# Turning the first four x tiles with plain identity products into fp32 PSUM, in place of transpose-mode instructions

## Chip, cores, metric

One core of a Trainium2 chip (trn2). The metric is the device time of one execution in microseconds (us), median over several executions. "Span" is the time from the first to the last instruction in one profiled execution; it is about 1.7 us shorter than the device time of the same run (163.9 against 165.6 us for the kernel before).

PE is the matmul engine (TensorE), DVE is VectorE, ACT is ScalarE, SP the engine that issues most DMAs (49 of 67 in the trace of the kernel before). PSUM (`ps` in the profiles) is the memory that PE's matmuls write here and that the evictions on DVE and ACT read.

## The reference

The reference mixes two branches of the same x (2048 x 512, bf16) with a gate:

```python
g = sigmoid((x * gate_w).sum(-1, keepdims=True))
a = A_ref(x, A_wqkv, A_wo)        # sliding, dilated attention; starts with x @ wqkv
b = B_ref(x, B_w1, B_b1, B_w2, B_b2)   # layer norm, then an MLP across tokens
return g * a + (1 - g) * b
```

Only `x @ wqkv` matters here. The kernel feeds these matmuls from x with the 512 features on the partitions, in four blocks of 128, that is, from x transposed.

## The kernel before

The kernel is emitted through a small list scheduler: each operation names the resources that it reads and writes ("b5" is PSUM bank 5), and the scheduler fixes an order per engine and the semaphore waits. The x tiles 4 to 15 are transposed by DMA. The first four are too urgent for that (in the trace before, the three DMA transposes land 5.9 to 8.7 us after their issue, the plain loads of x0 to x3 after 2.8 to 4.5): they are loaded plainly, turned on PE, and copied from PSUM to SBUF by DVE (tiles 0 and 2) and ACT (tiles 1 and 3).

```python
def f_warm(e):                      # PE work before any data has arrived
    for n_ in (512,) * 5 + (128,) * 4:
        ins = e.matmul(ps[:, 7, 0:n_], lhsT=C1, rhs=..., start=True, stop=True)

def f_tx(t, k_):                    # two 128x128 blocks of tile t into one bank
    def fn(e):
        for d_ in range(2):
            ins = e.transpose(out=psb(4 + 2 * (t % 2) + k_)[:, d_ * 128:d_ * 128 + 128],
                              in_=X[:, t, (2 * k_ + d_) * 128:(2 * k_ + d_ + 1) * 128], identity=IDENT)
        return ins
    return fn

def xt_ev(t, k_):                   # eviction of that bank to XT, as bf16
    eng = ("dve", "act")[t % 2]
    bk = 4 + 2 * (t % 2) + k_
    src = sub(psb(bk), 0, [(128, 2), (1, 128)])      # psb: the bank seen as bf16
    dst = sub(XT, 2 * k_ * S + t * 128, [(S, 2), (1, 128)])
    ...                             # tensor_copy on DVE, activation Copy on ACT

# ... cut: loads. Order of the DMA queues: x0 wq0 x2 wq2 (SP), x1 wq1 x3 wq3 (ACT), then wk0 wk1 wv x4.. (SP)
pe_tx(0)        # turn tiles 0 and 1: 8 blocks
pe_q0(0, 0)     # query products for their 256 tokens, feature block 0: 4 matmuls of 256 columns
pe_q0(0, 1)
pe_tx(2)        # turn tiles 2 and 3
pe_q0(0, 2)
pe_q0(1, 0); pe_q0(1, 1); pe_q0(1, 2)   # the 256 tokens of tiles 2 and 3
pe_q0(2, 3)     # feature block 3: 4 matmuls of 512 columns
# ... cut: key and value projections (512 columns each), attention, MLP, output
```

Of the kernel before, what the change touches and what calls it, by code (L numbers as in the profile page):

```python
# [280 lines left out]
class _Mem:  # L281
# [17 lines left out]
    def view(self, name, dtype, dims, extra=0, p0=0, np_=128):  # L299
        base = self.arena[:].bitcast(dtype)  # L300
        pst = base.ap[0][0]
        esz = mybir.dt.size(dtype)
        o = self.off[name]
        assert o % esz == 0
        return bass.AP(base.tensor, p0 * pst + o // esz + extra, [[pst, np_]] + [list(d) for d in dims])


def bass_gated_mix__sliding_local_dilated__mixer_token_mlp__prompt_kernel(nc, A_x, A_wqkv, A_wo, B_x, B_w1, B_b1, B_w2, B_b2, gate_w, out, dbg=None):
    with contextlib.ExitStack() as es:
# [37 lines left out]
        ps = es.enter_context(nc.psum_tensor("ps", [128, 8, 512], FP32))  # L347
# [11 lines left out]
        X = view("X", BF16, [(D, NST), (1, D)])  # L359
# [40 lines left out]
        IDENT = view("IDENT", BF16, [(1, 128)])  # L400
# [38 lines left out]
        def psb(bank):  # L439
            return ps[:, bank, :].bitcast(BF16)  # L440

        def sub(ap_, offs, dims):
            return bass.AP(ap_.tensor, ap_.offset + offs, [list(ap_.ap[0])] + [list(d) for d in dims])

        def psub(ap_, p0, np_, offs, dims):
            pst = ap_.ap[0][0]
            return bass.AP(ap_.tensor, ap_.offset + p0 * pst + offs, [[pst, np_]] + [list(d) for d in dims])
# [4 lines left out]
        def act(o_, i_, f_, **kw):  # L452
            return lambda e: e.activation(out=o_, in_=i_, func=f_, **kw)  # L453
# [109 lines left out]
        def f_tx(t, k_):  # L563
            def fn(e):
                ins = None
                for d_ in range(2):
                    ins = e.transpose(out=psb(4 + 2 * (t % 2) + k_)[:, d_ * 128:d_ * 128 + 128],  # L567
                                      in_=X[:, t, (2 * k_ + d_) * 128:(2 * k_ + d_ + 1) * 128], identity=IDENT)
                return ins
            return fn  # L570

# [2 lines left out]
        def xt_ev(t, k_):  # L574
            eng = ("dve", "act")[t % 2]
            bk = 4 + 2 * (t % 2) + k_
            src = sub(psb(bk), 0, [(128, 2), (1, 128)])
            dst = sub(XT, 2 * k_ * S + t * 128, [(S, 2), (1, 128)])
            extl[eng] = A(eng, (lambda e: e.tensor_copy(out=dst, in_=src)) if eng == "dve" else act(dst, src, AF.Copy),  # L579
                          0.27 if eng == "dve" else 0.35, reads=["b%d" % bk], writes=["xt0_%d_%d" % (t, k_)], name="ext%d_%d" % (t, k_), prio=-30)  # L580
# [12 lines left out]
        def pe_tx(t):  # L593
            for k_ in range(2):
                for t_ in (t, t + 1):
                    PE(f_tx(t_, k_), 0.2, ["x%d" % t_, "ident"], ["b%d" % (4 + 2 * (t_ % 2) + k_)], "tx%d_%d" % (t_, k_))
                    xt_ev(t_, k_)
# [133 lines left out]
        for h in range(2):  # L731
# [55 lines left out]
            for c in range(4):  # L787
                src = psub(ATT[h], 32 * c, 32, 0, [(0, 4), (1, NW * UT_)])
# [230 lines left out]
```

## Time and profile before

| | before |
|---|---|
| device time, 3 runs | 165.26 us (165.26 to 165.47) |
| span of the profiled run | 163.9 us |
| PE busy | 97% of the span |
| turning of the four tiles and first query products | 3.7 to 9.5 us |

From the page of the kernel before: the busy times (engine, us, share of the span, number of instructions), then the chain of work that ended last, by engine.

```profile
PE 159.3 (97%) x793; PEld 77.5 (47%) x808; DVE 150.7 (92%) x126; ACT 70.2 (43%) x100; POOL 12.0 (7%) x36
...
PE 95%; DMA 2%; ACT 1%; issue 1%; DVE 0%
```

PE is busy nearly throughout, and 95% of the chain is PE: what holds PE up lengthens the kernel. From the costliest groups of the same page (line, engine, operation, destination and source, count; then busy us and mean ns of one; then idle time before them and what ended it):

```profile
L579 DVE COPY arena<-ps 128x256 bf16<-128x256 bf16 x4 | 1.1, 291 | 4.4 <-PE ps L567 4.2
...
L588 PE MATMUL ps<-arena 128*128 128x256 bf16 (+1 forms) x27 | 4.4, 313 | 0.2
```

The evictions on DVE are bf16 to bf16, 291 ns each. The 27 query matmuls (24 of 256 columns, and three of the four of 512, one of which the trace lacks) average 313 ns, partly because some of them ran at a slow clock, as the next view shows. It is the timeline of the kernel before from 3.2 to 7.2 us, merged by line: start, length, engine, line, operation, count, and in brackets the idle time before it and what ended it. A group that runs on past 7.2 us is counted only up to there. PEld is the load of the stationary operand that goes ahead of a matmul (for the first query matmul at 4.86, ahead of 4.89 us).

```profile
3.74 1.01 PE L567 MATMUL ps<-arena 128*128 128x128 bf16 x8 [0.17 <-DMA arena<-in_A_x_dram]
4.15 0.72 DVE L579 COPY arena<-ps 128x256 bf16<-128x256 bf16 x2 [2.46 <-PE ps L567]
4.36 0.81 ACT L453 ACTIVATE arena<-ps 128x256 bf16<-128x256 bf16 x2 [0.37 <-PE ps L567]
4.86 1.37 PEld L588 LDWEIGHTS ps<-arena 128*128 128x128 bf16 x8 [0.38 <-DVE arena L579]
4.89 1.61 PE L588 MATMUL ps<-arena 128*128 128x256 bf16 x8
...
6.33 0.61 PE L567 MATMUL ps<-arena 128*128 128x128 bf16 x8
6.65 0.51 DVE L579 COPY arena<-ps 128x256 bf16<-128x256 bf16 x2 [1.78 <-PE ps L567]
...
6.76 0.66 ACT L453 ACTIVATE arena<-ps 128x256 bf16<-128x256 bf16 x2 [1.58 <-PE ps L567]
6.78 0.60 PE L588 MATMUL ps<-arena 128*128 128x256 bf16 x4
```

Read it as a staircase: eight transposes, evictions on DVE and ACT, eight query matmuls, eight transposes, evictions, more query matmuls. Single instructions of the same trace add three things. Transposes start 107 ns apart in the first group and 56 ns apart in the second. Query matmuls of 256 columns start 213 ns apart until about 6.1 us and 109 ns apart afterwards. "The clock doubles" is a name for this change below: it is read from the distances between starts, because the granted clock that the profile lists is 1.00 over these same first 10 us. And x0 landed at 3.60 us, x3 at 6.22, wq2 (the third block of the query weights) at 6.65.

### The profile page before, as it was taken

Reading aid. Unit: us, or ns where it says so; the run is one execution under the profiler, and the core shown is the slowest. Engines: PE = TensorE matmul, PEld = TensorE weight load, DVE = VectorE, ACT = ScalarE, POOL = GpSimd, SP = SyncE. Lnnn points to the kernel's source line nnn. Section 1 sums busy time; section 2 is a strip of 40 time slices with the busy share of each in tenths; the row PEclk is TensorE's granted clock in tenths of the full one; section 3 lists DMA queues with packets and bytes.
Section 4 is the critical chain, followed back from the end, with each engine's and each line's share of the span. In section 5 each row is a group of like instructions: output and inputs, shape, how many; then the busy total and the mean of one; then the engine's idle time right before and its main releaser. Section 6 shows DMA issues by size and latency. Waiting matters only on the chain.

```text
span 163.9 us, 1989 instructions
## 1 busy us (share of the span) xinstructions
PE 159.3 (97%) x793; PEld 77.5 (47%) x808; DVE 150.7 (92%) x126; ACT 70.2 (43%) x100; POOL 12.0 (7%) x36
## 2 busy tenths in 40 slices
PE   7999999999999999999999999999999999999993
PEld 3755555555544444444444344444444444444641
DVE  0589989999999999999999999999999999999971
ACT  3357677766672379753111258111121111111164
POOL 3000021020000000004000000002200222000000
DMA  4999969909499094999998974990998799991014
GB/s 153 288 233 253 254 128 291 199 11 188 91 304 308 1 247 120 256 290 290 298 263 233 270 203 142 298 232 10 283 254 192 185 204 201 211 222 38 32 58 135
DMA packets 44684, 32.24 MB, mean 197 GB/s; under 512 B 7940, under 2 KB 42244, under 8 KB 44676
## 3 DMA queue, kind: packets, MB, share of 16 engines
q1 hardware_dynamic: 41444, 22.06, 51.9%
q0 software_dynamic: 2512, 9.44, 27.2%
q10 hardware_dynamic: 720, 0.62, 1.1%
q8 instruction: 6, 0.10, 0.2%
q14 instruction: 2, 0.02, 0.0%
HBM read 18.88 MB, written 2.10 MB: 128 GB/s over the span
## 4 chain that ended last, share of the span: by engine, by line
PE 95%; DMA 2%; ACT 1%; issue 1%; DVE 0%
PE ps L858 29%; PE ps L885 29%; PE ps L649 23%; PE ps L894 8%; PE ps L588 3%; DMA arena<-in_A_x_dram 2%; PE ps L722 1%; ACT arena L453 1%; PE ps L567 1%; PE ps L717 1%; DVE arena L579 0%; PE ps L604 0%
## 5 line engine op out<-in xcount | busy, mean ns | idle before, releaser
L450 DVE TENSOR_TENSOR arena<-arena 128x4096 bf16<-128x4096 bf16 (+8 forms) x79 | 132.0, 1718 | 1.9 <-ACT arena L453 0.6
L885 PE MATMUL ps<-arena 128*128 128x512 bf16 (+2 forms) x234 | 50.0, 366 | 0.2
L858 PE MATMUL ps<-arena 128*128 128x512 bf16 x218 | 48.5, 379 | 0.3
L453 ACT ACTIVATE arena<-ps,arena 128x512 bf16<-128x512 f32 (+1 forms) x30 | 21.8, 731 | 60.7 <-PE ps L894 37.7
L453 ACT ACTIVATE arena<-ps 128x512 bf16<-128x512 f32 (+3 forms) x53 | 32.9, 629 | 18.3 <-PE ps L649 10.9
L649 PE MATMUL ps<-arena 128*128 128x512 bf16 x173 | 38.0, 379 | 0.2
L885 PEld LDWEIGHTS ps<-arena 128*128 128x128 bf16 x238 | 22.8, 98 | 25.9
L858 PEld LDWEIGHTS ps<-arena 128*128 128x128 bf16 x224 | 21.7, 98 | 26.8 <-issue 0.8
L649 PEld LDWEIGHTS ps<-arena 128*128 128x128 bf16 x176 | 19.9, 113 | 18.0
L894 PE MATMUL ps<-arena 128*128 128x512 bf16 (+2 forms) x67 | 15.6, 366 | 0.1
L453 ACT ACTIVATE arena<-arena 128x16 f32<-128x16 f32 (+5 forms) x10 | 6.7, 678 | 9.7 <-DVE arena L450 9.7
L692 DVE BATCH_NORM_STATS2 arena<-arena 128x6 f32<-128x512 bf16 x16 | 9.9, 679 | 0.5 <-DMA arena<-in_A_x_dram 0.5
L954 ACT ACT_TABLE_LOAD x7 | 9.0, 1283 | 2.8 <-issue 2.7
L894 PEld LDWEIGHTS ps<-arena 128*128 128x128 bf16 x68 | 6.5, 98 | 7.3
L790 POOL DMA_DIRECT2D arena<-arena x8 | 4.3, 556 | 75.2 <-DVE arena L450 75.2
L706 DVE TENSOR_SCALAR arena<-arena 128x512 bf16<-128x512 bf16 x16 | 5.3, 406 | 0.0
L579 DVE COPY arena<-ps 128x256 bf16<-128x256 bf16 x4 | 1.1, 291 | 4.4 <-PE ps L567 4.2
L827 POOL DMA_DIRECT2D arena<-arena x3 | 3.6, 1209 | 17.7 <-DVE arena L450 17.7
L747 POOL DMA_DIRECT2D arena<-arena x2 | 2.5, 1268 | 31.5 <-DVE arena L692 21.5
L588 PE MATMUL ps<-arena 128*128 128x256 bf16 (+1 forms) x27 | 4.4, 313 | 0.2
L588 PEld LDWEIGHTS ps<-arena 128*128 128x128 bf16 x28 | 3.1, 119 | 1.1 <-DVE arena L579 0.4
L551 PE MATMUL ps<-const-bfloat16-1.0 128*128 128x512 bf16 (+1 forms) x9 | 2.7, 483 | 0.8 <-PEq L1004 0.8
(30 smaller groups left out, 14.4 us busy)
## 6 DMA issues: line engine op xcount, KB each, us to landing
arena<-in_B_w_dram SPq DMA_DIRECT2D x7, 1024.0 KB, 6.5
arena<-in_B_w_dram SPq DMA_DIRECT2D x8, 896.0 KB, 9.9
arena<-arena POOLq DMA_DIRECT2D x5, 1024.0 KB, 10.0
arena<-arena POOLq DMA_DIRECT2D x8, 512.0 KB, 11.7
out_dram<-arena SPq DMA_DIRECT2D x15, 128.0 KB, 2.3
arena<-in_A_x_dram SPq DMA_DIRECT2D x3, 512.0 KB, 4.7
arena<-in_A_wqkv_dram SPq DMA_DIRECT2D x2, 256.0 KB, 4.3
arena<-in_A_wqkv_dram SPq DMA_DIRECT2D x1, 512.0 KB, 6.5
```

Source lines behind the costliest of these rows:

```text
L450: return lambda e: e.tensor_tensor(out=o_, in0=a_, in1=b_, op=op_)
L453: return lambda e: e.activation(out=o_, in_=i_, func=f_, **kw)
L588: ins = e.matmul(ps[:, dl, c0:c1], lhsT=sub(WQKV, dt * 3 * D + dl, [(4, 128)]), rhs=XT[:, dt, c0:c1], start=(dt == 0 and hb == 0), stop=(d ...
L649: ins = e.matmul(ps[:, bank, :], lhsT=sub(WQKV, dt * 3 * D + tn * D + dl, [(4, 128)]), rhs=XT[:, dt, sb * 512:(sb + 1) * 512], start=(dt = ...
L692: A("dve", (lambda t_: lambda e: e.bn_stats(out=ST6[:, t_, :], in_=X[:, t_, :]))(t), 0.67, reads=["x%d" % t], writes=["st%d" % t], name="s ...
L706: A("dve", (lambda t_: lambda e: e.tensor_scalar(out=X[:, t_, :], in0=X[:, t_, :], scalar1=col(RSTD, t_), scalar2=col(NMR, t_), op0=ALU.mu ...
L790: prev = sch.dma("pool", (lambda d_, s_: lambda e: e.dma_start(d_, s_))(dst, src), 524288, sch.dsem("av%d_%d" % (h, c)), issue=1.0, reads= ...
L827: sch.dma("pool", (lambda o_, i_: lambda e: e.dma_start(o_, i_, accum_op=ALU.add, max_dma_last_dim=4096))(pw(0, 4), pw(4, 4)), 1800000, sc ...
L858: ins = e.matmul(ps[:, bank, :], lhsT=W1H[ft // 2][:, st, 128 * (ft % 2):128 * (ft % 2) + 128], rhs=X[:, st, :], start=(st == 0), stop=(st ...
L885: ins = e.matmul(ps[:, bank, 0:c1 - c0], lhsT=W2S[i // 2][:, ft, 128 * (i % 2):128 * (i % 2) + 128], rhs=UT[:, ft, c0:c1], start=(ft == 0) ...
L894: ins = e.matmul(ps[:, bank, 0:c1 - c0], lhsT=OT[:, i // 2, dl, 128 * (i % 2):128 * (i % 2) + 128], rhs=WO[:, dl, c0:c1], start=False, sto ...
L954: e.preload_act_table_set(want)
```

## The change

The intent: write the turned tiles as ordinary fp32 products with the identity as the other operand (the run e2 of the changed kernel was checked as correct). The change also doubles the bytes that DVE and ACT read: sources of 128x256 bf16 before and 128x256 f32 after.

```diff
-                    ins = e.transpose(out=psb(4 + 2 * (t % 2) + k_)[:, d_ * 128:d_ * 128 + 128],
-                                      in_=X[:, t, (2 * k_ + d_) * 128:(2 * k_ + d_ + 1) * 128], identity=IDENT)
+                    ins = e.matmul(ps[:, 4 + 2 * (t % 2) + k_, d_ * 128:d_ * 128 + 128],
+                                   lhsT=X[:, t, (2 * k_ + d_) * 128:(2 * k_ + d_ + 1) * 128], rhs=IDENT, start=True, stop=True)
 ...
-            src = sub(psb(bk), 0, [(128, 2), (1, 128)])
+            src = sub(ps[:, bk, :], 0, [(128, 2), (1, 128)])
```

## The prediction

> **What bounds the kernel now.** TensorE. The page has PE busy 97% of a 163.9 us span, and the chain that ended last is 95% PE. From 9.5 us on, the timeline shows matmuls back to back. Only a shift of its start moves the end.
>
> **The stretch of the change** (timeline, single instructions): x0 lands at 3.60 us; eight transposes start at 3.74 (start to start 107 ns), then PE waits until 4.89; eight query matmuls of 256 columns follow, 213 ns apart until about 6.1 us and 110 ns after it (the clock doubles there); eight more transposes from 6.34 (56 ns apart); the other query matmuls from 6.78, with one short wait before 7.29. The DMA list has x2 landing at 5.91, x3 at 6.22, wq2 at 6.65, wq3 at 6.81.
>
> **What the change does.** The order stays on all five engines.
> - PE: 16 transposes become 16 plain matmuls, same stationary tile, same 128 moving columns. The warm-up's plain 128-column matmuls are 107 ns apart and take 311 ns at the slow clock, exactly as the transposes; fast ones of 256 and 512 columns, 109 and 216 ns apart, put one of 128 at about 56. Cost 0.
> - ACT: four copies of 256 elements, now fp32. Its bf16 one takes 383 ns, its fp32 512 one 597 ns: 0.84 ns per element joins them, so the type seems not to matter. Cost 0.
> - DVE: four copies of 290 ns [...] 512 fp32 take 691 ns. Estimate for 256: about 425 ns, +135 each, +0.54 us in all.
>
> **How much is critical.** Both PE waits end with ACT's copies. At 4.89, ACT's first copy ends at 4.75, DVE's at 4.44, which becomes 4.58: still earlier. At 7.29, ACT ends at 7.14, DVE at 6.94, which becomes 7.07: still earlier, by only 0.07 us. DVE's second copies are needed only at 6.50 and 8.05. The layer-norm statistics begin about 0.26 us later, push DVE's first eviction from 9.66 to about 9.8, and end in DVE's 0.64 us wait before 11.58. Nothing reaches the end.
>
> **The clock.** [...] If they bring the fast clock before 6.1 us, the first eight query matmuls could save up to 0.6 us on PE; but x3 at 6.22 and wq2 at 6.65 hold what follows, so at most 0.1 us gets through. A later doubling would cost half its delay. No run shows this yet.
>
> **Predicted time:** 165.3 us, 164.8 to 165.8 with 80%. Faster by over 2%: 1%; within 2%: 98%; slower by over 2%: 1%.
>
> **What would show each step.** Right: plain products 107/56 ns apart; ACT copies 383 ns; DVE copies about 425 ns; PE's waits end at 4.9 and 7.3 as before; DVE's first large multiply still starts near 11.6; PE's continuous stretch starts within 0.2 us of 9.46. Wrong: plain products spaced wider or ending later; DVE's copy above 0.5 us, so that PE waits for DVE at 7.3.
>
> **What would make it wrong.** A clock that doubles a microsecond later or earlier (some tenths of a us); DVE's delay shifting a DMA that collides later. Neither makes 2% (3.3 us).

The forecast's sum is 0 on PE, 0 on ACT, +0.54 us on DVE of which nothing reaches the end, and at most 0.1 us from an earlier clock, so the time of the kernel before (165.26 us) stands as 165.3. The 425 ns, and with it the +135 and +0.54 us, the 0.07 us and the 0.26 us, are the author's estimate. In the clock's step "they" are the plain products, and that they bring the fast clock earlier is a supposition. Its other numbers are estimates from the trace before: up to 0.6 us agrees with six starts of query matmuls 110 ns apart in place of 213, and "half its delay" with the same ratio.

## The result

| | before | after |
|---|---|---|
| device time, median of 6 runs | 165.55 us (165.26 to 165.92) | 165.40 us (164.70 to 165.56) |
| ratio after / before | | 0.9982, 95% interval 0.9957 to 1.0006 |
| span of the profiled run | 163.9 us | 163.0 us |

Ratios here are the mean time of one kernel's fast runs over the mean of the other's of the same rounds, so they are not quite the ratio of the medians. All runs of both kernels were fast.

The predicted 165.3 us is within 0.1 us of the measured median. But the two profiled executions differ by 0.9 us, which is six times the difference of the medians. That has to be explained before the profile may be read as support for anything.

The page after, the same lines:

```profile
PE 158.6 (97%) x793; PEld 77.2 (47%) x808; DVE 151.1 (93%) x126; ACT 70.2 (43%) x100; POOL 12.0 (7%) x36
...
PE 97%; ACT 1%; issue 1%
```

```profile
L579 DVE CAST arena<-ps 128x256 bf16<-128x256 f32 x4 | 1.6, 422 | 3.2 <-PE ps L567 3.2
L588 PE MATMUL ps<-arena 128*128 128x256 bf16 (+1 forms) x27 | 3.8, 284 | 0.2 <-ACT arena L453 0.2
```

The DVE evictions are now casts from fp32 and take 422 ns in place of 291: the predicted rise (about 425). The timeline of the changed kernel over the same stretch:

```profile
3.44 0.99 PE L567 MATMUL ps<-arena 128*128 128x128 bf16 x8
3.85 0.85 DVE L579 CAST arena<-ps 128x256 bf16<-128x256 f32 x2 [2.16 <-PE ps L567]
4.06 0.79 ACT L453 ACTIVATE arena<-ps 128x256 bf16<-128x256 f32 x2
...
4.59 1.04 PE L588 MATMUL ps<-arena 128*128 128x256 bf16 x8 [0.16 <-ACT arena L453]
...
5.46 0.61 PE L567 MATMUL ps<-arena 128*128 128x128 bf16 x8
5.78 0.76 DVE L579 CAST arena<-ps 128x256 bf16<-128x256 f32 x2 [1.08 <-PE ps L567]
...
5.89 0.66 ACT L453 ACTIVATE arena<-ps 128x256 bf16<-128x256 f32 x2 [1.04 <-PE ps L567]
5.91 1.55 PE L588 MATMUL ps<-arena 128*128 128x256 bf16 x12
```

In the chain, the busy share says little new: its start now runs through the warm-up and not through x0's landing, because x0 came (3.30 us) before the warm-up had ended (3.57). In the timeline, the first group takes 0.99 us against 1.01, the second 0.61 against 0.61. Single instructions: the products start 107 ns and then 56 ns apart, as the transposes did. An ACT eviction takes 384 ns against 383. So PE and ACT pay nothing, and DVE pays 131 ns four times.

That DVE's extra work is absorbed shows at its first large multiply (line 450), first before, then after, each from the view of DVE alone:

```profile
11.58 2.29 DVE L450 TENSOR_TENSOR arena<-arena 128x4096 bf16<-128x4096 bf16 x1 [0.64 <-ACT arena L453]
10.72 2.29 DVE L450 TENSOR_TENSOR arena<-arena 128x4096 bf16<-128x4096 bf16 x1 [0.62 <-ACT arena L453]
```

Both times it waits for ACT, and it starts 0.87 us earlier in the changed kernel, as the dense stretch of projections does (below).

Where do the 0.9 us come from? Two places, and both are over before 5.5 us:

- x0 landed at 3.30 us and not 3.60, so everything on PE starts 0.30 us earlier (first block at 3.44 against 3.74, first query matmul at 4.59 against 4.89).
- The clock had doubled before 4.59 us and not at 6.1, so the first eight query matmuls occupy 0.87 us of starts in place of 1.44 (4.59 to 5.46 against 4.89 to 6.33): 0.57 us.

The sum is 0.87 us, and the first projection matmul of 512 columns (line 649) starts at 8.59 against 9.46: 0.87 us earlier. From there on the two traces run in parallel, 154.4 us to the end in both. The question for the experiments is whether the change brought the earlier clock, or chance did.

### The profile page after: what moved, and what is told of

Read it like the earlier page. It is cut to its first block, busy times and chain, and to the rows that moved or that the text cites. A ratio compares the mean times of both kernels' runs of the same rounds, so it can differ in the third digit from the quotient of the medians.

```text
span 163.0 us, 1989 instructions
## 1 busy us (share of the span) xinstructions
PE 158.6 (97%) x793; PEld 77.2 (47%) x808; DVE 151.1 (93%) x126; ACT 70.2 (43%) x100; POOL 12.0 (7%) x36
## 4 chain that ended last, share of the span: by engine, by line
PE 97%; ACT 1%; issue 1%
PE ps L858 30%; PE ps L885 30%; PE ps L649 23%; PE ps L894 8%; PE ps L588 2%; PE ps L551 2%; PE ps L722 1%; ACT arena L453 1%; PE ps L717 1%; PE ps L567 1%; PE ps L604 0%
## 5 line engine op out<-in xcount | busy, mean ns | idle before, releaser
L579 DVE CAST arena<-ps 128x256 bf16<-128x256 f32 x4 | 1.6, 422 | 3.2 <-PE ps L567 3.2
L588 PE MATMUL ps<-arena 128*128 128x256 bf16 (+1 forms) x27 | 3.8, 284 | 0.2 <-ACT arena L453 0.2
```

The source lines that it names most:

```text
L588: ins = e.matmul(ps[:, dl, c0:c1], lhsT=sub(WQKV, dt * 3 * D + dl, [(4, 128)]), rhs=XT[:, dt, c0:c1], start=(dt == 0 and hb == 0), stop=(d ...
```

## Experiments

**Theory (chance).** The change costs PE nothing, DVE's longer casts are hidden, and the difference between the profiled spans is the moment at which the clock doubled and at which x and wq tiles landed, both of which vary from run to run of the same kernel.

**Rival (the change).** Plain products would count towards the fast clock and transposes would not, so that the change would bring it earlier. No trace had shown this: it is a supposition, and e3 tests it.

The ranges of 4 to 7 us (moments) and 3 to 7 us (after the first PE work) in the expectations below, and the 8 us of e7, are estimates. The two traces at hand had the fast clock at 5.9 to 6.1 (before) and 4.1 to 4.6 us (after), that is, 5.1 to 5.3 and 3.3 to 3.7 us after PE's first matmul at 0.85.

### e1 and e2: each kernel again

No edit: e1 is the kernel before, timed against itself; e2 is the changed kernel.

> The kernel before, unchanged, timed against itself: a null control, and a second trace of it. Chance theory (the 0.9 us between the two profiled spans is the landing of the x tiles plus the phase of the clock): ratio 1.000, interval within 0.3% of it, single times spread over about 165.0 to 166.0; in the trace the clock may double anywhere from 4 to 7 us, and the first projection of 512 columns (9.46 us before, 8.59 us after) starts wherever x3, wq2 and the clock put it. Rival [...]: in this trace the clock doubles again near 6.1 us, clearly later than the 4.4 us of the changed kernel.

> The changed kernel again, a second trace of it. Chance theory: ratio 0.998 to 1.002, and the clock doubles somewhere between 4 and 7 us, not tied to 4.4. Rival: doubling again before about 4.6 us, and a ratio of 0.996 to 0.998 that the null control does not show.

Measured, against the same 11 runs of the kernel before (median 165.59 us):

| | median | ratio | 95% interval |
|---|---|---|---|
| e1, before again | 165.37 us (6 runs) | 0.9989 | 0.9962 to 1.0017 |
| e2, after again | 165.39 us (6 runs) | 0.9993 | 0.9970 to 1.0016 |

The kernel before differs from itself (0.9989) about as much as the changed kernel differs from it (0.9993 here, 0.9982 in the first comparison), and all three intervals include 1. Now the second traces, PE's timeline, first e1 (transposes):

```profile
3.64 0.61 PE L567 MATMUL ps<-arena 128*128 128x128 bf16 x8
4.59 1.04 PE L588 MATMUL ps<-arena 128*128 128x256 bf16 x8 [0.34 <-DVE arena L579]
5.46 0.84 PE L567 MATMUL ps<-arena 128*128 128x128 bf16 x8
6.13 2.84 PE L588 MATMUL ps<-arena 128*128 128x256 bf16 x20
```

then e2 (products):

```profile
3.68 0.70 PE L567 MATMUL ps<-arena 128*128 128x128 bf16 x8
4.72 1.04 PE L588 MATMUL ps<-arena 128*128 128x256 bf16 x8 [0.34 <-ACT arena L453]
5.80 0.68 PE L567 MATMUL ps<-arena 128*128 128x128 bf16 x8
6.45 2.80 PE L588 MATMUL ps<-arena 128*128 128x256 bf16 x20
```

In e1 the first eight transposes take 0.61 us, not 1.01: the kernel *with transposes* had the fast clock before its first transpose at 3.64 us. In e2 it came at the fourth product, 3.94 us. So the rival's expectation for e1 (again near 6.1 us) failed; its expected ratio for e2 (0.996 to 0.998) was not found either, though the interval does not exclude all of it. Its expectation that e2 doubles before about 4.6 us came true, and the chance theory missed too: it had named 4 to 7 us, and both traces came before 4. What counts against the rival is e1 and, below, e3.

The two traces show something else. In e1 the second group takes 0.84 us and not 0.61, because its third transpose waited for x3, which landed at 5.74 us. In e2 the second group waited for x2 (5.75) and x3 (5.92), and the query matmul at 6.45 for wq2 (6.40). The clock came early in both, and late data ate part of the gain.

### e3 and e4: a train of 96 of each

The warm-up is replaced by 96 transposes, or by 96 plain products, of 128 columns; nothing else runs on PE before them. The train now also waits for the identity, so it starts at 1.43 us and not at 0.85.

```diff
-            for n_ in (512,) * 5 + (128,) * 4:
-                ins = e.matmul(ps[:, 7, 0:n_], lhsT=C1, rhs=..., start=True, stop=True)
+            for n_ in range(96):
+                ins = e.transpose(out=psb(7)[:, 0:128], in_=C1, identity=IDENT)        # e3
+                ins = e.matmul(ps[:, 7, 0:128], lhsT=C1, rhs=IDENT, start=True, stop=True)  # e4 in its place
```

> The warm-up of nine plain products is replaced by 96 transposes of 128 columns (10.3 us at the slow clock); everything behind it is late by some 7 us on purpose. Chance theory (a transpose counts like any other matmul): their start-to-start falls from 107 to 56 ns after 3 to 7 us of the train, and the query matmuls behind it run 109 ns apart from the first. Rival (transposes do not count): all 96 stay 107 ns apart, and the first query matmuls are 213 ns apart.

> The same train with 96 plain products into fp32 in place of the transposes. Both theories: start-to-start falls from 107 to 56 ns after 3 to 7 us of the train. If it doesn't, neither theory of the clock holds.

PE's timeline of e3 (transposes):

```profile
1.43 7.45 PE L551 MATMUL ps<-arena,const-bfloat16-1.0 128*128 128x128 bf16 x96 [1.43 <-POOL arena L460]
8.72 0.61 PE L567 MATMUL ps<-arena 128*128 128x128 bf16 x8
```

and of e4 (products):

```profile
1.44 7.97 PE L551 MATMUL ps<-arena,const-bfloat16-1.0 128*128 128x128 bf16 x96 [1.44 <-POOL arena L460]
9.24 0.61 PE L567 MATMUL ps<-arena 128*128 128x128 bf16 x8
```

96 starts at 107 ns would be 10.3 us. Both trains are much shorter, and the blocks behind them take the fast 0.61 us. Single instructions: in e3 the transposes start 107 ns apart until 5.46 us and 56 ns apart from 5.54 on, in e4 the products change over at 6.53 to 6.62. Only transposes, each with its weight load, had run on PE in e3 before its clock doubled. The rival falls: with transposes alone the clock doubled after 4.1 us, against 5.1 us with products alone. (Whether the transpose or the load ahead of it is what counts, no run separates; the kernel before has both too.) Both trains also show that the two kinds cost PE the same, 107 ns slow and 56 ns fast. (Both runs are single looks of unknown state, and the whole kernels are late on purpose; their total times, 170.23 and 170.86 us, say nothing.)

### e5: DVE's copies doubled

The changed kernel, in which DVE reads each bank twice:

```diff
-(lambda e: e.tensor_copy(out=dst, in_=src)) if eng == "dve"
+(lambda e: [e.tensor_copy(out=scr, in_=src), e.tensor_copy(out=dst, in_=src)]) if eng == "dve"
```

(`scr` is a row of the output buffer that nobody uses at that time.)

> The changed kernel, in which DVE reads each of its four fp32 banks twice (the first time into a scratch row that nobody reads), so that its copies take about 0.77 us a pair in place of 0.42. If DVE's margin before ACT's copy is 0.07 us, as the prediction reckoned (fast clock; 0.2 us where the clock is slow), PE's wait between the first transposes and the first query matmul now ends with DVE and grows by about 0.3 us (first query matmul about 0.85 us after the last transpose starts, not 0.45 to 0.56); the wait before the second column half grows likewise unless a late DMA hides it. Whole time: +0.3 to +0.7 us, ratio about 1.002 to 1.004. If DVE's copies are far from the critical path, PE starts as before and the ratio is 1.000.

The edit adds a line, so 588 and 649 are 589 and 650 here. Measured: median 165.73 us (4 runs) against 165.47 (11 runs), ratio 1.0009, interval 0.9977 to 1.0041. So the time alone does not tell. The trace does. PE's timeline:

```profile
3.53 1.01 PE L567 MATMUL ps<-arena 128*128 128x128 bf16 x8
4.75 1.41 PE L589 MATMUL ps<-arena 128*128 128x256 bf16 x8 [0.21 <-DVE arena L580]
6.00 0.61 PE L567 MATMUL ps<-arena 128*128 128x128 bf16 x8
6.45 3.04 PE L589 MATMUL ps<-arena 128*128 128x256 bf16 x19
9.33 0.59 PE L650 MATMUL ps<-arena 128*128 128x512 bf16 x2
```

and DVE's:

```profile
3.94 1.42 DVE L580 CAST arena<-ps 128x256 bf16<-128x256 f32 x4 [2.24 <-PE ps L567]
6.31 1.42 DVE L580 CAST arena<-ps 128x256 bf16<-128x256 f32 x4 [0.96 <-PE ps L567]
...
10.03 1.27 DVE L626 TENSOR_SCALAR arena<-ps 128x512 bf16<-128x512 f32 x2
11.45 2.29 DVE L450 TENSOR_TENSOR arena<-arena 128x4096 bf16<-128x4096 bf16 x1 [0.16 <-ACT arena L453]
```

PE's wait before 4.75 now does end with DVE, but it grew little. DVE's second cast ended at 4.694 us and the query matmul started at 4.752, 58 ns later. ACT's copy had ended at 4.535. In the traces of before, after, e1 and e2, the seven waits of this kind that no late DMA hides (two per trace, one in e2) all end 145 or 146 ns after ACT's copy, so ACT alone would have given 4.68: growth 0.07 us, not 0.3. At the second wait DVE ended at 7.069, PE started at 7.127 (again 58 ns later); the gap between starts there is 349 ns against 178 in the undisturbed traces, 0.17 us more. In all, 0.24 us, below what the ratio can resolve.

So the direction was right and the size was not. An ACT copy is followed by a longer pause than a DVE copy (145 against 58 ns). In these traces the wait for ACT is a semaphore instruction of its own, recorded with 51 ns ahead of the weight load, while the wait for DVE sits on the weight load. That this extra instruction makes the difference fits the traces but was not tested. DVE's true margin at the second wait is therefore the 0.07 us that the prediction named plus 87 ns, about 0.15 us.

Further down, DVE's doubled work pushed its statistics to 7.65 and its first eviction of a query bank to 10.03, half a microsecond after ACT's first one at 9.53. Yet its first large multiply starts 2.12 us after PE's first line-650 matmul (11.45 less 9.33), exactly as in the kernel before (11.58 less 9.46) and in the changed one (10.72 less 8.59). It waits for ACT's key eviction, with 0.16 us of DVE idle left in place of 0.64. In this trace the absorption holds even with every DVE copy made twice.

### e6: later key weights

A try at the landings. In the kernel before, the two key-weight loads wait for x2's landing in place of x0's. The edit is made after scheduling, so no order on any engine changes. (That these loads take bandwidth from x2, x3 and wq2 was not shown.)

```diff
         est = sch.schedule()
+        for op in sch.ops:
+            if op.name in ("wk0", "wk1"):
+                op.deps.discard(xld[0])
+                op.deps.add(xld[2])
```

> The kernel before, with the two key-weight loads issued when x2 has landed and not when x0 has[...]. If the start of the dense stretch is set by these landings, x3 and wq2 land 0.3 to 0.8 us earlier than in the traces so far (5.3 to 6.2 and 5.8 to 6.6 us), and the wait for them goes; but wk0 then lands about 8.5 to 9.5 us and may become the new wait before the dense stretch, so the ratio may be 0.998 to 1.003. If the landings do not depend on these loads, x3 and wq2 land where they did.

Measured: median 166.04 us (165.09 to 166.95, 6 runs), ratio 1.0033, interval 0.9991 to 1.0074. x3 landed at 5.34 and wq2 at 5.74, PE did not wait for them, and the first line-649 matmul started at 8.56. But the changed kernel had 5.30 and 5.76 with the loads as they were, so one trace does not show that the edit brought this: inconclusive. The new wait came later than expected: wk0 landed at 8.00 us, before the dense stretch (expected 8.5 to 9.5, as a possible wait), and PE waited for loads farther back. What it cost is clear from PE's waits (waited by <- ended by: us in total, times, longest):

```profile
PE ps L649 <- DMA arena<-in_A_x_dram: 0.4, 1, 0.4
...
PE ps L649 <- DMA arena<-in_A_wqkv_dram: 0.3, 1, 0.3
```

The value weights landed at 12.30 and the last DMA-transposed x tiles at 24.04 us, and all these loads sit in one queue behind the delayed ones; the starts of PE's matmuls around these two waits are 0.41 and 0.52 us further apart than the usual 216 ns, which accounts for the 0.94 us that this trace loses in the table below. No gain is shown.

### e7 and e8: no warm-up

Both kernels without the warm-up, so that the turning of x0 is PE's first work.

```diff
-        PE(f_warm, 2.6, [], ["b7"], "warm")
+        pass
```

> The kernel before without its warm-up: its transposes are then the first work of PE. If transposes count for the clock, it doubles 3 to 7 us after the first one, so between about 6.8 and 10.5 us; the dense stretch starts later by half of the delay, at about 9.5 to 11 us. If they did not count, not before 8 us.

> The changed kernel without its warm-up. Both theories: the clock doubles between about 6.8 and 10.5 us. If transposes and products count alike, what separates this trace from the one before it is only where in that interval each falls.

Measured (single looks, so their state is unknown; the granted clock was 1.00 in both): with transposes the clock doubled at 7.1 us, 3.5 us after the first of them; with products at 8.4 to 8.5, 4.8 us after the first. The stretch of 512-column projections starts at 9.86 and 10.50, the times are 165.99 and 166.63 us. Both fall within the stated interval, in the order opposite to what the rival would want, and e7 came before the 8 us that the expectation had set for transposes that do not count. But eight query products ran among the transposes in both, so this pair is weaker evidence than the trains. It also shows what the clock is worth: with x0 at 3.5 us in both, the stretch starts at 8.81 us in e1 and at 10.50 in e8. In e8 none of this is waiting for late data: from the first query matmul at 4.81 us to the stretch its PE starts follow each other without a pause.

### All traces side by side

The moment of the fast clock is bracketed by two starts of single PE instructions, and "dense from" is the first projection matmul of 512 columns.

| trace | turned by | x0 landed | wq2 landed | clock doubled | dense from | span | span - dense |
|---|---|---|---|---|---|---|---|
| before | transposes | 3.60 | 6.65 | 5.9 to 6.1 | 9.46 | 163.87 | 154.41 |
| e1 | transposes | 3.50 | 5.95 | 3.3 to 3.6 | 8.81 | 163.29 | 154.48 |
| e6 | transposes | 3.23 | 5.74 | 4.0 to 4.1 | 8.56 | 163.91 | 155.34 (two late loads) |
| e7, no warm-up | transposes | 3.49 | 7.10 | 7.1 to 7.2 | 9.86 | 164.26 | 154.40 |
| after | products | 3.30 | 5.76 | 4.1 to 4.6 | 8.59 | 162.98 | 154.39 |
| e2 | products | 3.54 | 6.40 | 3.8 to 3.9 | 9.08 | 163.47 | 154.39 |
| e5, DVE twice | products | 3.39 | 6.38 | 5.4 to 5.6 | 9.33 | 163.72 | 154.39 |
| e8, no warm-up | products | 3.52 | 6.56 | 8.4 to 8.5 | 10.50 | 164.90 | 154.40 |

After the dense stretch has begun, every trace but e6 needs 154.4 to 154.5 us. So, e6 apart, all of the spread between these executions lies in the first 10.5 us. With the warm-up, transposes had the fast clock between 3.3 and 6.1 us and products between 3.8 and 5.6: the ranges overlap, and neither kind is earlier. Over all ten traces (these and the two trains), most of which have pauses on PE, it came about 2.6 us (e1) to 5.2 us (before) after PE's first work. A few traces of each cannot exclude a small shift, but e3 excludes the mechanism that was proposed for it, transposes that do not count. Whether they count a little less or more, one train of each cannot tell.

## Why the prediction was right

- **The time.** Predicted 165.3 us (164.8 to 165.8); measured 165.40. Right, and for the main reason given: no part of the change lies on the critical path. That the two agree within 0.1 us is no finer confirmation, since single runs after spread from 164.70 to 165.56 us. Three of its own signs, set as moments, were missed in the profiled run after: PE's waits ended at 4.59 and 6.42 us (4.9 and 7.3 were named), the large multiply started at 10.72 (near 11.6), the stretch at 8.59 (within 0.2 us of 9.46). The unchanged kernel misses them as well in e1 (4.59, 6.64, 10.94 and 8.81), so they were signs of one trace's landings and clock, not of the change. Measured against the stretch, the multiply kept its place.
- **PE at no cost.** Right: 107 and 56 ns between starts for transposes and products alike, in the changed kernel and in both trains.
- **ACT at no cost.** Right: 384 ns against 383.
- **DVE about 135 ns more per eviction.** Right: 422 ns against 291, for one copy. The step from 691 ns (512 elements) to 425 (256) was the estimate; the trace after bears it out. Behind another copy the next starts after 341 ns (after, 5.78 us on) and 223 ns (before, 6.65 us on), so back to back DVE pays about 118 ns more per copy and not 131.
- **Both PE waits end with ACT.** Right, by the ends of the copies and the constant 145 ns behind them. The timeline before puts the first wait before line 588 down to DVE (the PEld line at 4.86 names DVE, for which the weight load waits); single instructions decide, for DVE's copy had ended at 4.44 and ACT's at 4.75. **"Earlier by only 0.07 us" was mis-sized**: it compared the ends of two copies and left out that PE resumes 145 ns after ACT but 58 ns after DVE. The margin is about 0.15 us (e5).
- **Statistics 0.26 us later, first DVE eviction pushed to about 9.8, all absorbed before 11.58.** Right in kind. Set against the dense stretch, the statistics began 0.24 us later, the eviction only 0.03 us later (8.83 after, against 9.66 less 0.87 = 8.79) where 0.14 was predicted: consecutive statistics start 593 ns apart although each is recorded with 675, so DVE had more slack than the sum of lengths showed. The multiply did not move.
- **The clock.** This step was wrong twice, without harm to the time. Its premise (the rival of the experiments) fell in e3, where the clock doubled after 4.1 us of transposes alone. "At most 0.1 us gets through" was read from one trace's landings: in the profiled run after, x3 landed at 5.30 and wq2 at 5.76, not at 6.22 and 6.65, and all 0.57 us of the earlier clock got through. The bound depends on when data lands, which differed by 0.9 us between these two executions. What saved the estimate is that neither has to do with the change.
- **Left open.** Whether the change shifts the time by less than about 0.4%: the intervals reach from 0.9957 to 1.0016 for the changed kernel and from 0.9962 to 1.0017 for the kernel before against itself. The moment at which the clock doubled was observed, not controlled.

## What to carry to other kernels

Before reading a difference of less than one per cent off two profiles, profile the unchanged kernel again: here it alone moved by 0.6 us, through DMA landings and the moment at which the matmul clock doubled. Here four evictions of twice the bytes (422 against 291 ns on DVE) cost PE nothing, because both of its waits ended with ACT's copies; compare the moments at which the reader could resume, semaphore included (here 145 ns behind ACT's copy, 58 ns behind DVE's), not the ends of the producers. And a claim about a whole mechanism ("this instruction does not count") is best tested by a train of nothing else.
